# Batch 0 of a chunked attention kernel: dummy matmuls at TensorE's waits, memory values loaded by another queue, one pair of heads turned in another order

## The chip, the cores and the metric

The kernel runs on one core of a Trainium2 chip. The metric is the device time of one execution in microseconds, as the median over several executions. The core's engines run their own instruction streams and meet at semaphores: TensorE (PE in the profile, with its weight loads as PEld), VectorE (DVE), ScalarE (ACT), GpSimd (POOL) and SyncE (SP). POOL and SP issue the DMA transfers here, and sixteen DMA engines carry them.

## What is computed

Two stages follow each other. The first is attention in chunks of 32 queries for 4 batches and 8 heads of size 64, over 768 positions. Each chunk sees 8 memory rows, 16 positions to its left and 8 to its right. The second is a dense layer pair over all 3072 tokens with a sine activation between them.

```python
for c in range(24):                       # chunks of 32
    l, r = max(0, 32*c - 16), min(768, 32*c + 40)
    k_full = concat(mem_k, k[:, :, l:r]); v_full = concat(mem_v, v[:, :, l:r])
    a = softmax(q[:, :, 32*c:32*c+32] @ k_full.T / 8)
    out[:, :, 32*c:32*c+32] = a @ v_full
x = out as (3072, 512)                    # heads side by side
h = x @ w_in                              # 512 -> 2048
y = (h + sin(alpha * h)**2 / alpha) @ w_out   # 2048 -> 512
```

## The kernel before, in words

All instructions of an engine run in the order in which the program writes them; no scheduler moves them. The four batches go one after another, and the attention of a batch is woven with the second product of the batch before it (L517). Batch 0 has nothing to be woven with, so it has its own function, `attention_first`, and this is where the change lies.

Batch 0 works on pairs of heads, called pair 0 to 3 here (`hp` in the code). For each pair `turn_k` and `turn_q` put twelve TensorE transposes each (L234) into a PSUM bank. The keys are then copied to `kT` by ScalarE (L249, the middle) and VectorE (L242, the edges), the queries to `qT` by VectorE (L256). The eight memory keys of every head are turned once (L405), copied to `memkT` (L406) and spread over the windows of `kT` by `put_memk` (L200). `sc(hp)` makes the scores of a pair in two halves: in each, two matmuls write the mask (L328), eight add the products (L336), and ScalarE takes the exponential (L343). `pv` (L355) multiplies by the values in `vw`, VectorE normalizes (L361, L362), and `x` turns the result (L372), which ScalarE copies to `xT` (L375). `alphas` turns a small table (L601) and copies it (L602, L603). Then `ahead` begins the first dense product (L471).

`warm(n)` issues `n` matmuls of zeros, 128x512, into the bank that `single()` would hand out next (L323). PSUM has eight banks. At the start they are split by `plan`: ring `one` is bank 6 alone, ring `t` (the transposes) is banks 4, 5 and 7, ring `big` (scores) begins at banks 0 and 2. A ring with one bank hands out the same bank each time, so a `warm` waits until that bank has been read.

POOL issues nearly all loads, with conversion from fp32 to bf16, in this order: keys and queries of pairs 0 to 3, with the memory values of all four batches (`memv_st`, L564) between the queries of pair 2 and the keys of pair 3; then the edges of the value windows (L186, L187), the values of pairs 0 to 3 in two parts each (L180, L181), and `w_in` in five parts (L207), `w_out`, and batch 1's keys and queries. Completion semaphores go round in a ring of eight, so the n-th transfer that POOL issues waits for the landing of the one eight places ahead of it. SP issues the memory keys in fp32 (L552) and the alpha table (L553) at the start. Later, `send_memv(1)` has SP copy batch 1's memory values into its value windows by eight small transfers (L197), which wait for the landing of `memv_st`. `put_memv(0, ...)` does the same for batch 0 by one VectorE copy (L190).

Of the kernel before, what the change touches and what calls it, by code (L numbers as in the profile page):

```python
# [9 lines left out]
P = 128  # L10
# [4 lines left out]
F32 = mybir.dt.float32  # L15
# [27 lines left out]
def kernel(  # L43
# [12 lines left out]
    nc = tc.nc  # L56
    B, H, S, D = q.shape
# [15 lines left out]
    mlp = ctx.enter_context(tc.tile_pool(name="mlp", bufs=3))  # L73
# [7 lines left out]
    def plan(**sets):  # L81
        for kind, ring in sets.items():
            rings[kind] = list(ring)
# [14 lines left out]
    def single(kind="one"):  # L98
        return ps[:, take_bank(kind), :]

    def packed(bank, n, width):
        return bank.bitcast(BF)[:, 0:n * width].rearrange("p (n c) -> p n c", n=n)

    plan(one=(6,), big=(0, 2), t=(4, 5, 7))

    ident = consts.tile([P, P], BF, name="ident")
    biasm = consts.tile([P, 6], F32, name="biasm")
# [9 lines left out]
    memv_st = consts.tile([P, B, H, D], BF, name="memv_st")  # L117
# [54 lines left out]
    def load_v(b, parts=((0, H),)):  # L172
        vw = vws[b % 2][:].rearrange("p h j c -> p (h j) c")
        vf = v[b].rearrange("h (j t) d -> t (h j) d", t=QW)
        n = H * NJ
        if len(parts) > 1:
            load_v_edges(vw, vf, n)
        for h0, h1 in parts:
            c0, c1 = h0 * NJ, h1 * NJ
            nc.gpsimd.dma_start(vw[16:64, c0:c1, 0:D], vf[0:48, c0:c1])  # L180
            nc.gpsimd.dma_start(vw[72:120, c0:c1, 0:D], vf[48:96, c0:c1])  # L181
        if len(parts) == 1:
            load_v_edges(vw, vf, n)

    def load_v_edges(vw, vf, n):
        nc.gpsimd.dma_start(vw[0:16, 1:n, 0:D], vf[80:96, 0:n - 1])  # L186
        nc.gpsimd.dma_start(vw[120:128, 0:n - 1, 0:D], vf[0:8, 1:n])  # L187

    def put_memv(b, eng, h0, h1):
        eng.tensor_copy(  # L190
            vws[b % 2][64:72, h0:h1, :, 0:D],
            memv_st[64:72, b, h0:h1, :].unsqueeze(2).to_broadcast([NM, h1 - h0, NJ, D]),
        )
# [5 lines left out]
    def put_memk(b):  # L199
        nc.vector.tensor_copy(  # L200
            kTs[b % 2][:, :, 24:856].rearrange("p g (j c) -> p g j c", c=104)[:, :, :, 40:40 + NM],
            memkT[:, :, NM * b:NM * b + NM].unsqueeze(2).to_broadcast([P, HP, NJ, NM]),
        )
# [23 lines left out]
    def turn(src, hp, pr):  # L227
        t = packed(single("t"), 6, P)
        for r in range(6):
            if pr is not None:  # L230
                nc.tensor.transpose(t[:, r, :], pr[:, r].rearrange("p e d -> p (e d)"), ident[:])
            else:
                for e in range(2):
                    nc.tensor.transpose(  # L234
                        t[64 * e:64 * e + 64, r, :], src[:, 2 * hp + e, r, :], ident[:]
                    )
        return t

    def put_k_edges(b, hp, t):
        kT = kTs[b % 2]  # L240
        for t0, c0 in ((0, 16), (120, 800)):
            nc.vector.tensor_copy(  # L242
                kT[:, hp, c0:c0 + 48].rearrange("p (a r) -> p a r", r=6),
                t[:, :, t0:t0 + 8].rearrange("p r a -> p a r"),
            )

    def put_k(b, hp, t):
        kT = kTs[b % 2]
        nc.scalar.copy(  # L249
            kT[:, hp, 72:72 + 7 * 104].rearrange("p (s c) -> p s c", c=104)[:, :, 0:96]  # L250
            .rearrange("p s (a r) -> p s a r", r=6),
            t[:, :, 8:120].rearrange("p r (s a) -> p s a r", a=16),
        )

    def put_q(b, hp, t, scalar=False):
        (nc.scalar.copy if scalar else nc.vector.tensor_copy)(  # L256
            qTs[b % 2][:, hp, :].rearrange("p (a r) -> p a r", r=6),
            t.rearrange("p r a -> p a r"),
        )
# [60 lines left out]
    def warm(n):  # L320
        z = ps[:, rings["one"][0], :]
        for _ in range(n):
            nc.tensor.matmul(z, idle[:, 0:P], idle[:])  # L323

    def unit_scores(hp, half):
        sc = two()
        for e in range(2):
            nc.tensor.matmul(  # L328
                sc[:, e, 0:4 * QW].rearrange("p (j m c) -> p j m c", j=4, m=3), ident[:],
                biasb[:, half].unsqueeze(3).to_broadcast([P, 4, 3, 32]),  # L330
                start=True, stop=False,
            )
        for jj in range(4):
            j = 4 * half + jj
            for e in range(2):
                nc.tensor.matmul(  # L336
                    sc[:, e, QW * jj:QW * jj + QW],
                    kTs[0][64 * e:64 * e + 64, hp, 104 * j:104 * j + P],
                    qTs[0][64 * e:64 * e + 64, hp, QW * j:QW * j + QW],
                    start=False, stop=(jj == 3),  # L340
                )
        pt = pt_first[:, 2 * hp + half, :]
        nc.scalar.activation(  # L343
            pt[:, 0:H * QW].rearrange("p (e c) -> p e c", e=2), sc[:, :, 0:4 * QW],
            ACTF.Exp, scale=0.125,
        )
        return pt
# [21 lines left out]
    def unit_turn(xT, hp, half, x_blk):  # L369
        xtp = packed(single(), 4, QW)  # L370
        for jj in range(4):
            nc.tensor.transpose(  # L372
                xtp[:, jj, :], x_blk[:, jj].rearrange("p e d -> p (e d)"), ident[0:QW, 0:QW]
            )
        nc.scalar.copy(  # L375
            xT[:, hp, HALF * half:HALF * half + HALF].rearrange("p (j c) -> p j c", j=4), xtp
        )

    def attention_first(kq, alphas, ahead):
        xT = xp.tile([P, KT, S], BF, name="xT")  # L380
        pt, xb = {}, {}

        def turn_k(hp):
            t = turn(kq[0], hp, None)
            put_k(0, hp, t)
            put_k_edges(0, hp, t)

        def turn_q(hp):
            put_q(0, hp, turn(kq[1], hp, None))

        def sc(hp):
            for half in range(2):
                pt[hp, half] = unit_scores(hp, half)

        def pv(*u):
            xb[u] = unit_values(*u, pt[u])

        def x(*u):
            unit_turn(xT, *u, xb.pop(u))

        turn_k(0)
        turn_q(0)
        mt = packed(single(), HP, 32)
        for g in range(HP):
            nc.tensor.transpose(mt[:, g, :], memk_bf[0:32, 2 * g:2 * g + 2, :].rearrange("p e d -> p (e d)"), ident[0:32, 0:32])  # L405
        nc.vector.tensor_copy(memkT[:], mt)  # L406
        put_memk(0)
        warm(2)
        turn_k(1)
        sc(0)  # L410
        turn_q(1)
        alphas()
        warm(1)
        turn_k(2)
        sc(1)
        turn_q(2)
        put_memv(0, nc.vector, 0, H)
        turn_k(3)
        sc(2)
        turn_q(3)  # L420
        sc(3)
        nc.scalar.preload_act_table(ACTF.Sin)
        send_memv(1)
        plan(big=(4, 0, 2), one=(6, 7))
        units = [(hp, half) for hp in range(HP - 1) for half in range(2)]
        pv(0, 0)
        for n in range(1, len(units)):
            warm(1)
            pv(*units[n])
            warm(1)  # L430
            x(*units[n - 1])
        warm(1)
        pv(3, 0)
        x(2, 1)
        pv(3, 1)
        x(3, 0)
        ahead(0, 0, xT)
        ahead(1, 0, xT)
        x(3, 1)
        ahead(2, 0, xT)  # L440
        return xT
# [108 lines left out]
    alpha_rows = consts.tile([FT, P], F32, name="alpha_rows")  # L550
    for bb in range(B):
        nc.sync.dma_start(memk_f[NM * bb:NM * bb + NM], mem_k[bb].rearrange("h n d -> n h d"))  # L552
    nc.sync.dma_start(alpha_rows[:], moe_alpha.rearrange("(ft p) -> ft p", p=P))  # L553
    nc.vector.memset(idle[:], 0.0)
    warm(8)
    for vw in vws:
        nc.vector.memset(vw[0:32, 0, 0, 0:D], 0.0)  # L557
        nc.vector.memset(vw[96:128, H - 1, NJ - 1, 0:D], 0.0)
# [1 line left out]
    masks.make_identity(nc, ident[:])  # L560
    for hp in range(1, HP):
        load_qk(0, kq, 2 * hp, 2 * hp + 2)
        if hp == 2:
            nc.gpsimd.dma_start(memv_st[64:72].rearrange("n b h d -> n (b h) d"),  # L564
                                mem_v.rearrange("b h n d -> n (b h) d"))
    load_v(0, [(2 * hp, 2 * hp + 2) for hp in range(HP)])
    for kT in kTs:
        nc.vector.memset(kT[:, :, 0:16], 0.0)
        nc.vector.memset(kT[:, :, 848:856], 0.0)
# [17 lines left out]
    nc.vector.tensor_copy(biasb[:, 0, 0, 0:1], biasm[:, 3:4])  # L587
    nc.vector.tensor_copy(biasb[:, 1, 3, 2:3], biasm[:, 4:5])
    nc.vector.tensor_copy(memk_bf[:], memk_f[0:32])
    nc.vector.tensor_copy(ident_f[:], ident[0:FT, 0:FT])  # L590
    nc.vector.memset(pt_first[:, :, H * QW:H * QW + 32], 0.0)
    for pt in pts:
# [61 lines left out]
    for pc in range(2 * HP):  # L654
        hp = pc % HP
        if pc + 3 < 2 * HP:
            prs.append(pair_up(kq1[(pc + 3) // HP], (pc + 3) % HP))
        t = turn(None, hp, prs[pc])
# [74 lines left out]
```

## Time and profile before

| | us |
|---|---|
| median of 7 runs | 228.16 |
| lowest, highest | 227.99, 231.42 |
| the profiled execution, its time | 228.70 |
| its span, first to last instruction | 226.9 |
| TensorE busy in the span | 212.3 (94%) |
| start of batch 0's first transposes (L234) | 5.46 |
| start of its first scores (L328) | 9.34 |
| start of its first values (L355) | 20.93 |
| start of the first dense product (L471) | 28.19 |

Times inside the profile count from the first instruction. "Start" rows come from the timeline of TensorE's instructions. A row of the timeline gives the start, the length of the group, the engine, the line, what it writes and reads, how many instructions, and in brackets the idle time ahead of it with what ended it. A row of the table by windows gives, for a stretch of time, each engine's busy time with its number of instructions, then the mean clock that TensorE was granted (1.00 is full), the DMA share and the GB/s moved.

### The profile page before, as it was taken

Reading aid. Unit: us, or ns where it says so; the run is one execution under the profiler, and the core shown is the slowest. Engines: PE = TensorE matmul, PEld = TensorE weight load, DVE = VectorE, ACT = ScalarE, POOL = GpSimd, SP = SyncE. Lnnn points to the kernel's source line nnn. Section 1 sums busy time; section 2 is a strip of 40 time slices with the busy share of each in tenths; the row PEclk is TensorE's granted clock in tenths of the full one; section 3 lists DMA queues with packets and bytes.
Section 4 is the critical chain, followed back from the end, with each engine's and each line's share of the span. In section 5 each row is a group of like instructions: output and inputs, shape, how many; then the busy total and the mean of one; then the engine's idle time right before and its main releaser. Section 6 shows DMA issues by size and latency. Waiting matters only on the chain.

```text
span 226.9 us, 4419 instructions
## 1 busy us (share of the span) xinstructions
PE 212.3 (94%) x1703; PEld 115.2 (51%) x1703; DVE 135.2 (60%) x237; ACT 151.8 (67%) x222; POOL 84.4 (37%) x106
## 2 busy tenths in 40 slices
PE   6787899999998999999989999999999999999993
PEld 2354655554545656554555555554555555554441
DVE  5437938885615869996783577654853764762110
ACT  2367568894687749999865787798948678660011
POOL 8877926596989971168770000000000000000000
PEclk9799999999999999999999999999999999999999
DMA  5999999999999999999999954532330100102212
GB/s 81 149 140 127 198 207 209 204 199 121 69 184 150 155 132 120 161 123 171 162 174 104 83 105 93 103 108 92 71 111 0 49 20 26 46 16 82 92 46 92
DMA packets 94629, 25.96 MB, mean 114 GB/s; under 512 B 82688, under 2 KB 91536, under 8 KB 94608
## 3 DMA queue, kind: packets, MB, share of 16 engines
q0 software_dynamic: 71648, 14.82, 106.0%
q1 hardware_dynamic: 22960, 10.86, 22.9%
q8 instruction: 13, 0.21, 0.4%
q14 instruction: 8, 0.07, 0.2%
HBM read 29.67 MB, written 6.29 MB: 158 GB/s over the span
## 4 chain that ended last, share of the span: by engine, by line
PE 54%; DVE 8%; ACT 2%; issue 2%; DVEq 0%; ACTq 0%
PE ps L517 29%; PE ps L471 20%; DVE gT L501 3%; PE ps L270 2%; PE ps L296 2%; DVE u L498 2%; DVE x_blk L303 1%; ACT u L491 1%; PE ps L313 1%; ACT u L495 1%; DVE xT L316 1%; ACT o_sb L532 0%; DVE rinv L302 0%; DVE o_sb L530 0%; DVEq L501 0%
## 5 line engine op out<-in xcount | busy, mean ns | idle before, releaser
L517 PE MATMUL ps<-w_out_sb,gT 128*128 128x512 bf16 x384 | 99.2, 379 | 2.4 <-DVE o_sb L530 0.8
L471 PE MATMUL ps<-xT,w_in_sb 128*128 128x384 bf16 x512 | 90.0, 326 | 0.7 <-DVE gT L501 0.7
L501 DVE SCALAR_TENSOR_TENSOR gT<-u,inv_alpha,ps 128x768 bf16<-128x768 f32 x64 | 63.3, 1011 | 24.2 <-ACT u L495 20.1
L491 ACT ACTIVATE u<-ps,alpha_sb 128x768 f32<-128x768 f32 x64 | 57.0, 898 | 22.3 <-PE ps L471 21.2
L471 PEld LDWEIGHTS <-w_in_sb 128*128 128x128 bf16 x512 | 49.7, 98 | 37.5 <-issue 2.0
L517 PEld LDWEIGHTS <-gT 128*128 128x128 bf16 x384 | 34.3, 97 | 32.7 <-issue 2.7
L495 ACT ACTIVATE u<-u 128x768 f32<-128x768 f32 x40 | 33.7, 843 | 1.2
L283 ACT ACTIVATE pt<-ps,biasm 128x256 bf16<-128x256 f32 x72 | 28.7, 476 | 6.0 <-ACT pt L283 2.3
L530 DVE COPY o_sb<-ps 128x512 f32<-128x512 f32 x12 | 8.2, 687 | 24.5 <-PE ps L517 24.5
L532 ACT COPY o_sb<-ps 128x512 f32<-128x512 f32 x12 | 7.1, 588 | 22.2 <-PE ps L517 22.2
L498 DVE TENSOR_TENSOR u<-u 128x768 f32<-128x768 f32 x18 | 17.8, 988 | 6.0 <-ACT u L491 5.9
L303 DVE TENSOR_TENSOR x_blk<-ps,rinv 96x512 bf16<-96x512 f32 x24 | 16.5, 687 | 1.0 <-DVE rinv L302 0.2
L144 POOL DMA_DIRECT2D kst<-in_k_dram x16 | 11.7, 731 | 7.2 <-DMA vw<-in_v_dram 3.6
L139 POOL DMA_DIRECT2D kst<-in_k_dram x16 | 11.1, 693 | 7.8 <-DMA vw<-in_v_dram 6.2
L249 ACT COPY kT<-ps 128x672 bf16<-128x672 bf16 x8 | 5.8, 719 | 12.1 <-PE ps L234 8.6
L302 DVE RECIPROCAL rinv<-ps 96x8 f32<-96x8 f32 x24 | 4.9, 203 | 12.1 <-PE ps L296 6.2
L323 PE MATMUL ps<-idle 128*128 128x512 bf16 x22 | 8.7, 469 | 3.3 <-DVE vw L557 1.2
L498 POOL TENSOR_TENSOR u<-u 128x768 f32<-128x768 f32 x6 | 8.9, 1494 | 7.6 <-ACT u L491 7.6
L296 PEld LDWEIGHTS <-pt 128*128 128x128 bf16 x192 | 9.0, 98 | 4.8 <-issue 0.8
L152 POOL DMA_DIRECT2D qst<-in_q_dram x12 | 10.6, 898 | 1.4 <-DMA kst<-in_k_dram 1.2
L296 PE MATMUL ps<-vw,pt 128*128 128x65 bf16 x192 | 9.8, 193 | 0.0
L270 PEld LDWEIGHTS <-kT 64*128 64x128 bf16 x192 | 4.9, 94 | 7.6 <-issue 7.0
(76 smaller groups left out, 153.5 us busy)
## 6 DMA issues: line engine op xcount, KB each, us to landing
out_dram<-o_sb SPq DMA_DIRECT2D x24, 256.0 KB
vw<-in_v_dram POOLq DMA_DIRECT2D x6, 384.0 KB, 12.2
w_out_sb<-in_moe_w_out_dram POOLq DMA_DIRECT2D x2, 1024.0 KB, 17.7
w_in_sb<-in_moe_w_in_dram POOLq DMA_DIRECT2D x3, 512.0 KB, 9.6
qst<-in_q_dram POOLq DMA_DIRECT2D x12, 128.0 KB, 6.4
kst<-in_k_dram POOLq DMA_DIRECT2D x14, 64.0 KB, 5.3
kst<-in_k_dram POOLq DMA_DIRECT2D x14, 56.0 KB, 5.7
k_bf<-in_k_dram POOLq DMA_DIRECT2D x4, 192.0 KB, 5.5
```

Of the source, the lines that this page charges most:

```text
L139: nc.gpsimd.dma_start(kst[r0:64, j, :].rearrange("p (h d) -> p h d", d=D), k[b, :, lo + r0:lo + 64, :].rearrange("h p d -> p h d"),)
L144: nc.gpsimd.dma_start(kst[72:72 + n, j, :].rearrange("p (h d) -> p h d", d=D), k[b, :, QW * j + 48:QW * j + 48 + n, :].rearrange("h p d -> ...
L152: nc.gpsimd.dma_start(qst[:, t, :].rearrange("p (h d) -> p h d", d=D), q[b, :, P * t:P * t + P, :].rearrange("h p d -> p h d"),)
L283: nc.scalar.activation(pt[:, 0:H * QW].rearrange("p (g e c) -> p g e c", g=2, e=4)[:, :, :, 32 * m:32 * m + 32], sc[:, :, 0:4 * QW].rearra ...
L296: nc.tensor.matmul(otv[:, e, hp, :], pt[:, QW * i:QW * i + P], vws[b % 2][:, 2 * hp + e, j, 0:D + 1],)
L303: nc.vector.tensor_tensor(out=x_blk[:].rearrange("p g e d -> p e g d"), in0=otv[0:QW, :, :, 0:D], in1=rinv[:].unsqueeze(3).to_broadcast([Q ...
L471: nc.tensor.matmul(hT[:, hf, 0:HALF], w_in_sb[:, kt, P * ft:P * ft + P], xT[:, kt, HALF * hf:HALF * hf + HALF], start=(kt == 0), stop=(kt ...
L491: nc.scalar.activation(u[:], hT[:, :, 0:HALF], ACTF.Sin, scale=alpha_sb[:, ft:ft + 1])
L495: nc.scalar.activation(u[:], u[:], ACTF.Square)
L498: eng.tensor_tensor(out=u[:], in0=u[:], in1=u[:], op=ALU.mult)
L501: nc.vector.scalar_tensor_tensor(out=gT[:, ft, :].rearrange("p (e c) -> p e c", e=2), in0=u[:], scalar=inv_alpha[:, ft:ft + 1], in1=hT[:, ...
L517: nc.tensor.matmul(ps[:, bank, :], gT[:, ft, P * s:P * s + P], w_out_sb[:, ft, :], start=(ft == 0), stop=(ft == FT - 1),)
```

## The change

Four things change, all ahead of or in batch 0.

1. Ring `one` gets banks 6 and 7, and ring `t` keeps 4 and 5.
2. More `warm` calls: 11 at the start where there were 8; two after the first keys' transposes; three after `put_memk` where there were two; two ahead of the first scores; two after `alphas` where there was one; two after `turn_k(2)`; four after `turn_k(3)`; two ahead of the last scores.
3. SP loads the memory values of batch 0 as fp32 (`memv_f`, behind the memory keys and ahead of the alpha table), and VectorE converts them. POOL loads those of batches 1 to 3 behind the values. `put_memv(0)` stands behind `alphas` and no longer behind `turn_q(2)`.
4. The last pair's queries (`turn_q(3)`) are turned ahead of the scores of pair 2, and no longer behind them.

```diff
-    plan(one=(6,), big=(0, 2), t=(4, 5, 7))
+    plan(one=(6, 7), big=(0, 2), t=(4, 5))
...
         turn_k(0)
+        warm(2)
         turn_q(0)
         mt = packed(single(), HP, 32)
...
         put_memk(0)
+        warm(3)
+        turn_k(1)
         warm(2)
-        turn_k(1)
         sc(0)
         turn_q(1)
         alphas()
-        warm(1)
+        put_memv(0, nc.vector, 0, H)
+        warm(2)
         turn_k(2)
+        warm(2)
         sc(1)
         turn_q(2)
-        put_memv(0, nc.vector, 0, H)
         turn_k(3)
+        warm(4)
+        turn_q(3)
         sc(2)
-        turn_q(3)
+        warm(2)
         sc(3)
...
         nc.sync.dma_start(memk_f[NM * bb:NM * bb + NM], mem_k[bb].rearrange("h n d -> n h d"))
+    memv_f = mlp.tile([P, H, D], F32, name="memv_f", tag="o_sb", bufs=2)
+    nc.sync.dma_start(memv_f[64:72], mem_v[0].rearrange("h n d -> n h d"))
     nc.sync.dma_start(alpha_rows[:], moe_alpha.rearrange("(ft p) -> ft p", p=P))
     nc.vector.memset(idle[:], 0.0)
-    warm(8)
+    warm(11)
...
     for hp in range(1, HP):
         load_qk(0, kq, 2 * hp, 2 * hp + 2)
-        if hp == 2:
-            nc.gpsimd.dma_start(memv_st[64:72].rearrange("n b h d -> n (b h) d"),
-                                mem_v.rearrange("b h n d -> n (b h) d"))
     load_v(0, [(2 * hp, 2 * hp + 2) for hp in range(HP)])
+    nc.gpsimd.dma_start(memv_st[64:72, 1:B].rearrange("n b h d -> n (b h) d"),
+                        mem_v[1:B].rearrange("b h n d -> n (b h) d"))
...
     nc.vector.tensor_copy(memk_bf[:], memk_f[0:32])
+    nc.vector.tensor_copy(memv_st[64:72, 0], memv_f[64:72])
     nc.vector.tensor_copy(ident_f[:], ident[0:FT, 0:FT])
```

## The prediction, as it was put on record

> **What bounds the kernel now.** I read the page first, for TensorE's share and its clock; then TensorE's timeline up to the first dense product; then the table by windows over that stretch; then the issues of each transfer, one by one, with their time to landing. The page says that TensorE is 94% busy over the span and that the only slices below full clock are at its head:
>
> ```profile
> PE   6787899999998999999989999999999999999993
> PEclk9799999999999999999999999999999999999999
> ```
>
> So after batch 0 the kernel is a chain of dense matmuls, and a change in batch 0 is worth what it moves the start of that chain (28.19 us). In the table by windows, cut where the clock changes, the reader is to see one stretch of 3.41 us at half clock, behind a stretch of equal length in which TensorE was busy for only 1.95 us:
>
> ```profile
> core 0: us, PE busy (x) PEld busy (x) DVE busy (x) ACT busy (x) POOL busy (x), PEclk, DMA share, GB/s
> 0.00:5.45 5.45, 3.59 (x8) 1.01 (x8) 3.08 (x24) 1.28 (x1) 4.32 (x11) 1.00 0.55 79
> 5.45:8.86 3.41, 1.95 (x36) 1.27 (x38) 2.52 (x14) 0.72 (x1) 3.41 (x6) 1.00 1.14 156
> 8.86:12.27 3.41, 3.41 (x44) 1.71 (x40) 0.32 (x2) 1.98 (x3) 2.52 (x4) 0.50 1.23 148
> 12.27:15.68 3.41, 2.43 (x40) 1.23 (x36) 1.61 (x5) 1.55 (x3) 2.84 (x5) 1.00 2.63 144
> ```
>
> TensorE's own timeline shows the idle places, with what ended each:
>
> ```profile
> 8.15 0.59 PE L323 MATMUL ps<-idle 128*128 128x512 bf16 x2 [1.00 <-DVE memkT L406]
> 8.68 0.73 PE L234 MATMUL ps<-ident,k_bf 128*64 128x128 bf16 x12
> 13.62 0.38 PE L323 MATMUL ps<-idle 128*128 128x512 bf16 x1 [0.98 <-DVE alpha_sb L602]
> 13.92 0.53 PE L234 MATMUL ps<-ident,k_bf 128*64 128x128 bf16 x12
> 17.38 0.35 PE L336 MATMUL ps<-qT,kT 64*128 64x96 bf16 x8 [0.29 <-DVE qT L256]
> 19.94 0.35 PE L336 MATMUL ps<-qT,kT 64*128 64x96 bf16 x8 [0.62 <-DVE qT L256]
> 20.93 0.42 PE L355 MATMUL ps<-vw,pt_first 128*128 128x65 bf16 x8
> ```
>
> The two waits of about 1.0 us are zero matmuls that wait for their single bank to be read (memkT, alpha_sb), and everything is queued behind them. Landings, as issue plus time to landing, in us: keys of pair 1 3.40+4.6 = 8.0, queries of pair 1 4.12+6.1 = 10.2, keys 2 4.83+6.5 = 11.3, queries 2 5.54+7.1 = 12.6, keys 3 6.93+6.4 = 13.3, queries 3 7.64+7.2 = 14.8; second parts of the values: pair 0 11.66+7.1 = 18.8, pair 1 13.63+8.4 = 22.0, pair 2 15.10+8.4 = 23.5, pair 3 17.71+6.8 = 24.5; first part of w_in 18.91+6.6 = 25.5, second 19.66+7.1 = 26.8.
>
> **The change part by part.** Unit prices from the timeline, start to start at full clock: twelve transposes 0.46 (13.92 to 14.38), followed directly by others 0.37 to 0.43; a pair's scores 1.41 (14.38 to 15.79); a zero matmul 0.21 (21.18 to 21.39 between values). At half clock the scores took 2.37 (9.34 to 11.71).
>
> *Start.* The first eight zero matmuls are 0.427 apart (weight loads at 2.02, 2.45, 2.88, 3.30, 3.73). Eleven put the last at 1.19 + 10 x 0.427 = 5.46, just when the first keys land; they then start at about 5.7 instead of 5.46 (0.4 late if the last three run slow). Keys 0 5.7, two zero matmuls 6.1, queries 0 6.55 (landed at 6.34), memory keys 7.0, three zero matmuls 7.2: these no longer wait for memkT, because ring `one` has a second bank. They end at 7.85, and keys 1 start at their landing, 8.0 against 8.68.
>
> *VectorE beside it.* It gets one cast more, of 8 partitions x 512; its nearest row is the memk_bf cast of the same length, 0.53. At 5.8 it pushes the key edges from 6.78 to 7.3, the query copy (0.95) to 7.5, memkT to 8.4 and put_memk to 8.6, done at 8.95. Scores 0 need that at 9.33 (below), and keys 1, which now share a bank with keys 0, need the edges done by 8.0: covered by 0.4. The cast waits for SP's transfer. SP's queue shows memory keys and alpha moved by 5.5 (the last three packets of its queue lie in 5.0 to 5.5); the new transfer takes alpha's place, so I take no wait; the far bound is the 6.6 us that POOL's memory values took to land, 2.2+6.6 = 8.8.
>
> *Middle.* Keys 1 8.0, zeros 8.45, scores 0 8.9 to 10.3, queries 1 (landed 10.2) 10.3, alpha 10.75, zeros 10.95, keys 2 (landed 11.3) 11.36 against 13.92. Of these 2.56 us, 0.7 come from the memkT wait, about 1.2 from the clock (0.96 on scores 0, 0.24 on queries 1), and 1.0 from the alpha wait, less the zeros put in. Zeros 11.8, scores 1 12.25 to 13.65, queries 2 13.65, keys 3 14.1, four zeros 14.5, queries 3 15.36, scores 2 15.8 to 17.2, zeros, scores 3 17.65 to 19.06. From keys 2 on the stretch grows from 7.0 to 7.7: eight zeros cost 1.7, and the waits of 0.29 and 0.62 with their restarts go. No step waits: put_memv (1.22) now runs on VectorE at about 12.1 to 13.35, ahead of the key edges of pair 2 (to 13.6), which keys 3 need at 14.1 for the bank; the query copies end at 11.8, 15.1 and 16.8, needed at 12.7, 15.8 and 18.1; ScalarE's exponentials (0.76 each) keep pace. put_memv may hold up POOL's descriptor work for half a microsecond, as it did before (the issue beside it took 1.20, the others 0.73); POOL then waits for landings anyway.
>
> *Clock: a rule weighed.* The windows show the half clock behind a stretch with no idle gap above 1.00 us and 57% busy, and full clock kept behind 2.43 of 3.41 (71%). The Trainium skill, "TensorE: Matmul & The Clock Gate", section "Why this matters for your kernels", asks only that no idle gap be over about 3 us. By that rule the clock would not have fallen here at all, so zeros would buy no clock; the trace contradicts it, and I go with the trace. The same page's Part 4 says that transposes do not count as busy in the same way. That speaks against the change: counted so, the stretch before the fall had the 0.59 of zeros, and the one that kept the clock 2.43 less 0.9 of transposes, 1.5. The changed stretch has 0.2+0.43+0.64+0.4 = 1.7 without transposes, and over 3.2 with them: above both kept values. If the clock falls for one stretch all the same, scores 0 and queries 1 cost 1.2 more and the gain at the values is 0.6.
>
> *Loads and values.* POOL's order loses the 0.73 us issue of memory values ahead of keys 3, and each later transfer waits for the one eight ahead in the new count, so the first value parts go out some 1.4 earlier. But DMA has been full since 4 us (share above 1), so landings follow traffic. Ahead of pair 1's values go away 256 rows of memory values and SP's eight small copies (8 x 64 rows, issued 12.88 to 18.85, now behind the later load); 64 rows come in. Six value parts of 768 rows landed between 18.8 and 24.5: 1.24 ns a row, so 704 rows are 0.87 us. Pair 1's values then land at 21.1, within bounds of 20.9 and 22.0. Values 0 start at 19.06 (landed by 18.8), and pair 1's follow 1.84 later as before: 20.9 wanted, 21.1 had. So late next is a landing, by 0.2, and the gain at 22.76 is 1.65 (0.75 if no traffic is saved). The values of pairs 2 and 3 have 1.3 and 2.1 us before, and follow.
>
> *Behind it.* VectorE's pace of 0.85 to 1.07 a unit is unchanged, so the dense product starts near 26.6. w_in part 1 lands at 25.5 plus up to 0.6 for the copies now beside it (26.1); part 2 at 27.4, wanted at about 28.4. Batch 1's keys land at 48.4, wanted on POOL at 50.93, then 49.3; its queries at 52.6, wanted at 56.26; its values at 62.8 at the latest, wanted at 67.94. None is late by an advance of 1.6.
>
> Sum: 1.65 less a little lost in the chain, 1.5 us. The profiled execution took 228.70 with a span of 226.9; it would be 227.2. Its time is 0.54 above the median of the seven, so the median goes from 228.16 to 226.7.
>
> **The rivals.**
> *The landings bind.* If SP's copies and memory values took no DMA time from the values, pair 1 lands at 22.0 and the gain is 0.75: 227.4. For it: share well above 1 at 13 to 22 us, with many transfers under way; against: GB/s fall to about 80 to 120 while the copies are issued.
> *The clock falls still, or falls at another place.* Its stretches need not lie at the same places in other executions. Gain 0.6: 227.5. Two such stretches: none, 228.7.
> *Slower: VectorE's queue stops at the new cast.* If memv_f lands late, the key edges, the query copy, memkT and put_memk wait, with them keys 1 and scores 0. From 6.2 on it eats the slack, at 7.8 the gain is gone, and at the 8.8 of the far bound scores 0 start 2.2 to 2.5 late with TensorE idle and the clock at half behind it (1.2): about 230.3. Against: the packets of SP's queue.
> *More than the sum.* The chain of values gains from the early activation-table load, and landings leave no wait: 2.3 or more, below 225.9.
> *That it does not act* is excluded by the order: the two waits are gone from the instructions.
>
> **How the numbers follow.** Sum 0.55, landings 0.15, clock 0.12, slower 0.07, more 0.11. What a measurement here tells from no change is about 1%, 2.28 us: faster means below 225.9, slower above 230.4. The sum and the first two rivals lie within it. So faster 0.11, same 0.83, slower 0.06. The range leaves out half of the faster case and the slower one: 225.9 to 228.2.
>
> **What would show it.** Right: granted clock 1.00 from 5.5 on; zeros directly behind the memory keys; keys 2 near 11.4; first values near 19.1; the dense product near 26.6. Wrong: an idle place on VectorE ahead of the new cast; a window at 0.50; values of pair 1 waiting for a DMA by more than 0.5; L471 waiting for w_in.

## The result and the profile after

| | before | changed |
|---|---|---|
| median of the comparison, us | 229.07 (61 runs) | 227.40 (24 runs) |
| lowest to highest | 227.98 to 231.69 | 226.78 to 228.44 |
| the profiled execution | 228.70 | 228.50 |

The ratio of changed to before is 0.9921, with a 95% interval of 0.9900 to 0.9943: 1.8 us less on 229. A second comparison gave medians of 228.70 and 227.21 and a ratio of 0.9955 (0.9938 to 0.9972). There, the ratio leaves out those runs of the kernel before that lie more than 1.5% above its fastest (226.56), so it is nearer to 1 than the medians are; both are given below.

The two profiles differ by only 0.2 us, since the changed kernel's is of an execution longer than all 24 of the comparison. Its profile still shows what the change did. First the table by windows of the changed kernel, cut where it was cut before:

```profile
core 0: us, PE busy (x) PEld busy (x) DVE busy (x) ACT busy (x) POOL busy (x), PEclk, DMA share, GB/s
0.00:5.45 5.45, 4.26 (x11) 1.49 (x11) 3.09 (x24) 1.28 (x1) 4.33 (x11) 1.00 0.53 78
5.45:8.86 3.41, 3.41 (x41) 1.60 (x41) 2.93 (x14) 0.72 (x1) 3.41 (x6) 1.00 1.17 166
8.86:12.27 3.41, 3.41 (x53) 1.75 (x51) 1.49 (x5) 2.24 (x3) 2.66 (x4) 1.00 1.18 157
12.27:15.68 3.41, 3.41 (x60) 2.03 (x61) 3.00 (x7) 2.51 (x4) 2.22 (x3) 1.00 3.07 129
```

TensorE is busy throughout, and no window is recorded at half clock. Then lines of TensorE's timeline, for the places that were idle before and for what is idle now:

```profile
6.00 0.85 PE L234 MATMUL ps<-ident,k_bf 128*64 128x128 bf16 x12
...
7.77 0.26 PE L406 MATMUL ps<-ident,memk_bf 32*128 32x32 bf16 x4
7.97 0.82 PE L323 MATMUL ps<-idle 128*128 128x512 bf16 x3
8.72 0.53 PE L234 MATMUL ps<-ident,k_bf 128*64 128x128 bf16 x12
...
12.18 0.53 PE L234 MATMUL ps<-ident,k_bf 128*64 128x128 bf16 x12
...
20.64 0.40 PE L355 MATMUL ps<-vw,pt_first 128*128 128x65 bf16 x8 [0.59 <-DMA vw<-in_v_dram]
...
27.79 1.70 PE L476 MATMUL ps<-xT,w_in_sb 128*128 128x384 bf16 x8
```

The zeros follow the memory keys without a wait (7.97), the second wait is gone too, and keys 2 start at 12.18 where they started at 13.92. But the first keys start at 6.00 and take 0.85 where they took 0.53, which is the duration at half clock (the last section shows how the record can miss it), and the first values wait 0.59 us for a landing. Of the 1.74 us that keys 2 had gained, 0.4 are left at the dense product (27.79 against 28.19).

### The profile page after: what moved, and what is told of

It reads as the page before. It is cut to its first block, busy times and chain, and to the rows that moved or that the text cites. A ratio compares the mean times of both kernels' runs of the same rounds, so it can differ in the third digit from the quotient of the medians.

```text
span 226.7 us, 4455 instructions
## 1 busy us (share of the span) xinstructions
PE 215.5 (95%) x1720; PEld 116.2 (51%) x1720; DVE 135.6 (60%) x238; ACT 151.7 (67%) x222; POOL 84.2 (37%) x106
## 4 chain that ended last, share of the span: by engine, by line
PE 40%; DMA 26%; POOL 13%; SPq 8%; issue 5%; DVE 4%; ACT 2%; POOLq 1%; DVEq 0%; ACTq 0%
PE ps L522 21%; DMA vw<-in_v_dram 17%; PE ps L476 14%; DMA kst<-in_k_dram 8%; SPq L159 4%; POOL qst L152 4%; SPq L162 4%; POOL kst L144 2%; DVE gT L506 2%; POOL kst L139 2%; POOL q_bf L167 1%; ACT u L496 1%; POOL k_bf L167 1%; DMA out_dram<-o_sb 1%; POOL vw L180 1%
## 5 line engine op out<-in xcount | busy, mean ns | idle before, releaser
L503 DVE TENSOR_TENSOR u<-u 128x768 f32<-128x768 f32 x18 | 17.2, 954 | 6.0 <-ACT u L496 5.9
L323 PE MATMUL ps<-idle 128*128 128x512 bf16 x39 | 13.9, 452 | 1.2 <-DVE vw L564 1.2
L152 POOL DMA_DIRECT2D qst<-in_q_dram x12 | 10.5, 902 | 0.8 <-DMA kst<-in_k_dram 0.8
## 6 DMA issues: line engine op xcount, KB each, us to landing
w_out_sb<-in_moe_w_out_dram POOLq DMA_DIRECT2D x2, 1024.0 KB, 18.6
```

The lines of the kernel that those rows point to most:

```text
L152: nc.gpsimd.dma_start(qst[:, t, :].rearrange("p (h d) -> p h d", d=D), q[b, :, P * t:P * t + P, :].rearrange("h p d -> p h d"),)
L503: eng.tensor_tensor(out=u[:], in0=u[:], in1=u[:], op=ALU.mult)
```

## The experiments

Each kernel ran beside the kernel before on one chip. "Mean clock" is the granted clock averaged over an execution; one stretch of 3.4 us at half clock makes it 0.992, since 1.7 of 227 us are lost. It does not count a head at half clock that lies ahead of the first recorded change (last section).

### Each part alone or left out

**The memory values alone** (part 3 of the change, nothing else).

```diff
+    nc.sync.dma_start(memv_f[64:72], mem_v[0].rearrange("h n d -> n h d"))
...
-        put_memv(0, nc.vector, 0, H)      # behind turn_q(2)
+        put_memv(0, nc.vector, 0, H)      # behind alphas()
```

> The kernel before with the memory-value edits alone (part 3 of the change). Theory A (the gain comes from TensorE's filled waits and its clock; the loads' new order gives nothing by itself): the half-clock stretch behind the first transposes stays, first values start at about 20.9 as before, pair 0's values land near 20.5 because more transfers share the DMA engines; time within 0.3 us of the kernel before, ratio 0.998 to 1.002. Theory B (the freed DMA traffic brings the values and through them the time): first values earlier by 0.5 or more and the time 0.9 us shorter, ratio 0.996.

Measured: median 229.73 against 228.99, ratio 1.005 (1.0018 to 1.0082). Both theories fall: it costs. Eight of its runs have a mean clock of 0.991 to 0.993, and the shortest of them (228.95) is longer than the longest of the twenty such runs of the kernel before (228.81). VectorE's timeline of this kernel:

```profile
5.26 0.53 DVE L590 CAST memk_bf<-memk_f 32x512 bf16<-32x512 f32 x1
5.82 0.69 DVE L591 CAST memv_st<-memv_f 8x512 bf16<-8x512 f32 x1
6.52 0.45 DVE L592 CAST ident_f<-ident 16x16 f32<-16x16 bf16 x1
...
8.43 0.20 DVE L406 COPY memkT<-ps 128x128 bf16<-128x128 bf16 x1
```

The new cast does not wait for its data, but it took 0.69 us where I had taken 0.53, and the small copy behind it 0.45 where it had taken 0.15. memkT is copied at 8.43 and not at 7.88, and the zeros, and keys 1 behind them, still wait for it. This looks like the cause, but the profile does not show it. In this execution the first queries are turned at half clock (0.85 for twelve transposes, 0.51 more up to the memory keys), so that their copy, which stands ahead of memkT's, could hardly have begun earlier. The kernel with the second bank alone (below) has no such cast, was profiled with the same half clock, and copies memkT later still:

```profile
8.51 0.21 DVE L406 COPY memkT<-ps 128x128 bf16<-128x128 bf16 x1
```

Keys 2 start at 14.89 here and at 13.92 in the kernel before, and nearly all of that is the half clock: 0.51 up to the memory keys, 0.53 on the zeros and keys 1. From keys 2 to the first values both take 7.0. Where the head runs at full clock, as in the profile of the kernel without the last six zeros (below), the cast does delay that copy: it starts 0.48 behind its transposes, against 0.06 in the kernel before. So about 0.4 us is an estimate of what the cast can cost while keys 1 wait for memkT; that it makes up the 0.5% is likely and not shown. The values do come earlier (pair 1's second part was issued at 12.54 and took 7.4 us: 19.9 against 22.0 before), but TensorE was not waiting for them.

**Everything but the memory values** (parts 1, 2 and 4).

```diff
-    nc.sync.dma_start(memv_f[64:72], mem_v[0].rearrange("h n d -> n h d"))
-    nc.vector.tensor_copy(memv_st[64:72, 0], memv_f[64:72])
...
+        if hp == 2:
+            nc.gpsimd.dma_start(memv_st[64:72].rearrange("n b h d -> n (b h) d"),
+                                mem_v.rearrange("b h n d -> n (b h) d"))
```

> The changed kernel without the memory-value edits: zeros, second bank and the order of the last queries alone. Theory A: clock at 1.00 throughout, put_memv now late on VectorE and in front of the last query copy (scores 3 about 0.5 later), pair 0's values land near 19 as before the change, pair 1's at 22.0; the gain over the kernel before is 0.75 to 1.8 us, ratio 0.992 to 0.997. Theory B (the memory-value edits carry the gain): ratio 0.998 to 1.000.

Measured: 227.12 (six runs, 226.67 to 227.38), ratio 0.9920 (0.9890 to 0.9949). All of the gain is there without part 3. Mean clock 0.997 or more in all six. In its profile pair 0's values landed at 20.0 and the first values wait 0.57 us for them, so this wait does not come from part 3 alone.

**The second bank alone** (part 1).

```diff
-    plan(one=(6,), big=(0, 2), t=(4, 5, 7))
+    plan(one=(6, 7), big=(0, 2), t=(4, 5))
```

> The kernel before with the second bank for the ring of single banks alone (the two waits of 1 us on the copies go, no zeros are added). Theory clock (what counts is that TensorE is kept busy so that its clock is not halved): the stretch of half clock of about 3.4 us is still there, scores 0 still take 2.4, and the gain is under 0.8 us, ratio 0.9965 or more. Theory waits (what counts are the waits of 1.0 and 0.98 themselves): keys 2 start 1.0 to 1.7 us earlier than 13.92 and the gain is 1.5 us or more, ratio 0.9935 or less.

Measured: 227.39 (226.12 to 229.47), ratio 0.9923 (0.9897 to 0.9949). One line brings as much at the median as the whole change, although the mean clock is 0.992 or lower in 15 of its 22 runs. From its timeline of TensorE:

```profile
7.52 0.28 PE L405 MATMUL ps<-ident,memk_bf 32*128 32x32 bf16 x4
7.74 1.03 PE L323 MATMUL ps<-idle 128*128 128x512 bf16 x2
8.70 0.85 PE L234 MATMUL ps<-ident,k_bf 128*64 128x128 bf16 x12
...
12.10 0.53 PE L234 MATMUL ps<-ident,k_bf 128*64 128x128 bf16 x12
...
19.83 0.40 PE L355 MATMUL ps<-vw,pt_first 128*128 128x65 bf16 x8 [0.67 <-DMA vw<-in_v_dram]
```

In this execution the keys of pair 1 still run at half clock (0.85), yet keys 2 start at 12.10, 1.82 us earlier than before and no later than in the changed kernel. The waits account for it: from the memory keys to the zeros behind them it is 0.22 where it was 1.26, and from alpha to keys 2 0.48 where it was 1.51, together 2.07 less. The half clock lies elsewhere in the two executions, earlier in this one, and takes back 0.25: 1.18 more up to scores 0, 0.93 less on scores 0 and queries 1. The reader should also see the last line: here too the first values wait for a landing, though this kernel's loads are those of the kernel before.

**The zeros alone** (part 2 with the single bank and the old order).

```diff
-    warm(8)
+    warm(11)
...
+        warm(2)                 # behind turn_k(0)
...
-        warm(2)
+        warm(3)                 # behind put_memk(0)
         turn_k(1)
+        warm(2)
...
-        warm(1)
+        warm(2)                 # behind alphas()
         turn_k(2)
+        warm(2)
...
+        warm(4)                 # behind turn_k(3)
...
+        warm(2)                 # ahead of sc(3)
```

> The kernel before with all the new zero matmuls, but with its single bank for them and its old order, so that the two waits of 1 us on the copies stay. Theory clock (the zeros' worth is a clock that does not fall): the mean granted clock of nearly every run is 0.995 or more where the kernel before has 0.992 or 0.978 in 32 of 43 runs, and the ratio is 0.992 to 0.997. Theory waits (the worth lies in the bank that takes the two waits away, the zeros are load on TensorE's path): ratio 0.998 or more, the zeros behind the last keys and ahead of the last scores showing as about 1 us more between keys 2 and the first values.

Measured: 229.37 against 228.70, ratio 1.0044 (1.0026 to 1.0061). The mean clock was 0.995 or more in 22 of 22 runs, as the clock theory said, and the time got longer, as the other said. Over all runs the means are 229.27 and 229.05: the zeros narrow the spread (228.33 to 229.93, against 226.56 to 231.56) and do not lower the middle. TensorE's timeline has both old waits in it, and zeros that come on top:

```profile
8.38 0.81 PE L323 MATMUL ps<-idle 128*128 128x512 bf16 x3 [0.99 <-DVE memkT L407]
...
13.08 0.59 PE L323 MATMUL ps<-idle 128*128 128x512 bf16 x2 [0.97 <-DVE alpha_sb L607]
13.61 0.53 PE L234 MATMUL ps<-ident,k_bf 128*64 128x128 bf16 x12
...
16.70 1.04 PE L323 MATMUL ps<-idle 128*128 128x512 bf16 x4
```

Keys 2 start at 13.61, only 0.3 earlier than before, with the clock whole; then the zeros behind keys 3 take 0.9 (16.70 to 17.58).

**Everything but the new zeros** (parts 1, 3 and 4, with the old 8, 2 and 1).

> The changed kernel with only the zeros that the kernel before has (8, 2 and 1). Theory clock: the clock falls in part of the runs (means of 0.992 or less in a third or more of them), the spread between lowest and highest is 2.5 us or more as with the ring alone (226.1 to 229.5), and the median is 227.2 to 228. Theory waits: no loss against the changed kernel, median 226.0 to 226.9, since its path is shorter by the zeros.

Measured: 226.99 (226.40 to 229.20, 16 runs); the changed kernel beside it 227.21. Ratio 0.9960 (0.9934 to 0.9986), median against median 226.99/228.70 = 0.9925. The mean clock fell to 0.988 to 0.992 in 5 of 16 runs, and the spread is 2.8 us. So the zeros do keep the clock whole and the runs together, but they do not shorten the median. In the execution profiled the first values wait 1.28 us for pair 0's landing, so there a shorter path of TensorE could not show.

### Fewer zeros, and the changed kernel again

**Without the last six** (four behind keys 3, two ahead of scores 3).

```diff
-        warm(4)
         turn_q(3)
         sc(2)
-        warm(2)
         sc(3)
```

> The changed kernel without the four zero matmuls behind the last keys and the two ahead of the last scores. Theory landing (in the changed kernel the first values wait for pair 0's landing at about 20.5, 0.6 us of wait in the profile): scores 3 end about 1 us earlier, the wait grows by as much, time same as the changed kernel within 0.3 us, ratio to before 0.991 to 0.9935. Theory TensorE (its own queue of work ends last): the first values come 0.9 to 1.3 earlier, ratio to before 0.987 or less.

Measured: 226.74 (226.59 to 227.37, six runs), ratio 0.9909 (0.9880 to 0.9939). In its profile the first values start at 19.02 with no wait, and pair 0's values had landed at 18.6. Neither theory holds as stated: the time is 0.7 below the changed kernel's 227.40, or 0.3 by the two ratios to the kernel before, and not 1.2, and the landing was not late in this execution. Leaving out six zeros, about 1.3 us of work, shortened the stretch from keys 2 to the first values by only 0.4 (11.60 to 19.02 here, 12.11 to 19.90 in the second profile of the changed kernel), since other waits take their place, the longest ahead of queries 3:

```profile
15.48 0.53 PE L234 MATMUL ps<-ident,q_bf 128*64 128x128 bf16 x12 [0.72 <-DVE qT L256]
```

**Zeros only where TensorE waits anyway.**

```diff
-    warm(11)
+    warm(10)
...
         turn_k(1)
-        warm(2)
         sc(0)
...
         turn_k(2)
-        warm(2)
         sc(1)
...
-        warm(4)
         turn_q(3)
         sc(2)
-        warm(2)
```

> The changed kernel with zeros only where TensorE has to wait for a landing or a copy anyway: ten at the start (the last then ends as the first keys land), two behind the first keys, three behind the memory keys, two behind alpha, none ahead of scores 0, 1, 3 and none behind the last keys. If the zeros that fill no wait are pure load: 226.1 to 226.6, ratio 0.987 to 0.990, clock 0.995 or more in all runs. If they are needed for the clock: means of 0.992 in part of the runs and a median of 226.9 or more.

Measured: 226.87 (226.16 to 228.36), ratio 0.9906 (0.9880 to 0.9932), median against median 0.9920; the changed kernel beside it 227.21. The two ratios, 0.9906 and 0.9955, are further apart than these medians, which are 0.34 us apart. 21 of 22 runs have a mean clock of 0.995 or more, so those few zeros hold the clock. The median is above my 226.1 to 226.6. The execution profiled is one of the longest (228.19) and shows two waits, 1.06 us ahead of the first values for pair 0's landing and 1.05 at 153.12 (see "Behind it" below); how much of them is in the median is not shown.

**The changed kernel once more.**

> The changed kernel as it is, beside the others on one chip, with a second profile. Its first profile was one of its slowest executions: first keys still at half clock, pair 0's values landed at 20.5 and TensorE waited 0.59 us for them. If these two are what makes its runs differ, a profile at about 227.2 shows first keys at full clock, keys 2 near 11.6 and pair 0's values landing by 19.5 with first values at 19.2 to 19.8; if landing is always late, the wait of about 0.6 is there again with first values at 20 or later.

Measured: 227.21 (226.71 to 227.72, 22 runs). In this profile pair 0's second part went out at 10.46 and took 9.0 us: landed at 19.46, first values at 19.90 without a wait, dense product at 27.16. The first keys are at 6.00 again. So the late start is the same in both profiles and the late landing is not. The late start is not fixed either: with the same eleven zeros, the profiles of the zeros alone and of the kernel without the last six have the first keys at 5.57 and 5.58, at full clock (0.53).

### The landing

In both profiles of the changed kernel pair 0's values are issued earlier than before and land later. These are the DMA issues of the kernel before and then of the changed kernel, each for a stretch in which only this transfer is issued; the last figure is the time to landing:

```profile
vw<-in_v_dram POOLq DMA_DIRECT2D x1, 96.0 KB, 7.1
```

```profile
vw<-in_v_dram POOLq DMA_DIRECT2D x1, 96.0 KB, 10.5
```

Issued at 11.66 it landed at 18.8; issued at 10.01 it landed at 20.5. An early issue alone does not do it: with the memory values alone this part was issued at 10.52 and landed at 18.6. Nor does it take the new loads: with the second bank alone, 11.24 and 19.7. If rows that lie ahead of it in the queue delay it, then taking some away should help. The edges of the value windows are 1512 rows for all pairs, of which pair 0 needs a quarter.

```diff
         if len(parts) > 1:
-            load_v_edges(vw, vf, n)
+            load_v_edges(vw, vf, n, 0, n // 2)
         for h0, h1 in parts:
+            if 2 * h0 == H:
+                load_v_edges(vw, vf, n, n // 2, n)
```

> The kernel with zeros only at the waits, and with the edges of the value windows loaded in two halves: those of pairs 0 and 1 ahead of pair 0's values, those of pairs 2 and 3 behind pair 1's. It takes 756 of 1512 edge rows out of the traffic ahead of pair 0's values and adds two issues on the load queue. Theory landing (the first values of the changed kernel wait for pair 0's landing at 19.5 to 20.5, and rows ahead of it are what delays it): pair 0 lands at 18.5 to 19.0, the wait of 1.06 us ahead of the first values is under 0.4, median 225.9 to 226.4 against 226.87. Theory sharing (transfers under way at the same time share the DMA engines, so that an earlier place in the queue brings nothing): landing and wait as before, median 226.7 to 227.1.

Measured: 226.18 (225.84 to 226.75, six runs) against 229.11, ratio 0.9893 (0.9856 to 0.9929). Pair 0 landed at 18.05 (issued 9.75, 8.3 to landing). Where the kernel with the same zeros but whole edges has the first line, this one has the second:

```profile
19.62 0.40 PE L355 MATMUL ps<-vw,pt_first 128*128 128x65 bf16 x8 [1.06 <-DMA vw<-in_v_dram]
```

```profile
18.52 0.42 PE L359 MATMUL ps<-vw,pt_first 128*128 128x65 bf16 x8
```

The wait of 1.06 us is gone, and the median is 0.7 lower, though measured on another chip; the intervals of the two ratios overlap (0.9893 here, 0.9906 there), so the gain in time is not shown.

**The same with the old memory values.**

> The same with the memory values loaded and copied as in the kernel before, so without the new cast on VectorE and with SP's small copies again beside the values. If the memory-value edits bring the values earlier: pair 0's values land 0.5 to 1 us later than with them and the median is 0.4 to 0.8 us above the one with them. If they bring nothing: the same within 0.3 us.

Measured: 225.85 (225.21 to 226.41, six runs), ratio 0.9882 (0.9847 to 0.9917), the shortest of all here. Without part 3 the time is, if anything, shorter. Pair 0 landed at 18.5 (issued 11.11, 7.4 to landing). The two landings with split edges lie below all ten profiles with whole edges, 18.6 to 20.5. In its profile the next wait is the one that the prediction had looked for and not found in the changed kernel, the first part of w_in:

```profile
26.78 1.47 PE L476 MATMUL ps<-xT,w_in_sb 128*128 128x384 bf16 x8 [0.77 <-DMA w_in_sb<-in_moe_w_in_dram]
```

| kernel | median | before, same runs | ratio (95%) |
|---|---|---|---|
| second bank alone | 227.39 | 228.99 | 0.9923 (0.9897 to 0.9949) |
| zeros alone | 229.37 | 228.70 | 1.0044 (1.0026 to 1.0061) |
| memory values alone | 229.73 | 228.99 | 1.0050 (1.0018 to 1.0082) |
| whole change, second comparison | 227.21 | 228.70 | 0.9955 (0.9938 to 0.9972) |
| bank, order, few zeros, split edges | 225.85 | 229.11 | 0.9882 (0.9847 to 0.9917) |

## Why the prediction was right, and where its reasons were not

**The total.** 1.5 us less was forecast; the medians of the two comparisons differ by 1.67 and 1.49. 226.7 against 227.40 is mostly the kernel before, whose median was 229.07 over 61 runs and not 228.16 as over seven. That the sum came out is in part luck: the lead was to be 2.56 at keys 2 and 1.6 at the dense product, and the two profiles had 1.74 and 1.81, then 0.40 and 1.03. What the parts below lost came back in places that the prediction had not named, and in runs of the kernel before that were longer than the one it was read from.

**The waits on one bank: right.** Both are gone, and the second bank alone carries the gain (0.9923). I had booked 0.7 and 1.0 for them; the bank alone took 2.07 from them, 1.82 at keys 2.

**The clock: the mechanism right, its worth wrong.** The term "about 1.2 from the clock" was read from one execution as if every one had that half-clock stretch and lost that much by it. The zeros do keep the recorded clock (0.996 or more in all 47 executions of the changed kernel), but added alone they made the kernel 0.4% slower. The runs of the kernel before with just one such stretch are, by their median, its shortest (below). The limit between 57% and 71% busy was read from one execution, and no run here tests it. And the filler has its price, though less than "eight zeros cost 1.7" suggests: leaving out six brought 0.4 on TensorE's path, since VectorE's copies then set the pace.

**The start: mis-sized.** I had the first keys at 5.7. Eleven zeros that are all at half clock (0.427 each) end at 5.9, and the keys behind them can be at half clock as well: 6.00 in both profiles, with 0.85 and 0.79 for twelve transposes. This is most of the 0.8 by which keys 2 (12.18) missed the forecast 11.36.

**The new cast: the price was low, the cover held.** It took 0.69 and not 0.53. Part 3 alone costs 0.5%, and whether through the cast is not shown; in the changed kernel nothing on TensorE waits for it, since keys 1 no longer stand behind memkT. The rival in which VectorE stops for a late transfer did not occur: there is no idle time ahead of the cast.

**The landings: a step that failed.** "Values 0 start at 19.06 (landed by 18.8)" took an earlier issue and less traffic to mean a landing no later than before. It was 20.5 and 19.5 in the two profiles, with time to landing up from 7.1 to 10.5 and 9.0. What came late was pair 0; I had expected it of pair 1. That rows ahead of it are part of the cause fits the two profiles with split edges, which land below all others; with so few, and times that overlap, it is not settled. Why the same transfers land a microsecond apart in two executions of one kernel stays open. So does the worth of the 0.87 us of freed traffic: leaving part 3 out made no difference that these runs can tell (227.12 against 227.40 and 227.21).

**Behind it: right for the loads it named, incomplete for the rest.** w_in was in time, but the lead at the dense product is not what arrives at the end. In the second profile it is 1.03 at 27.16, 1.64 at 118, and 1.2 at the end, 0.4 of it going behind the last copy. The gain on the way is a wait of the kernel before that shrinks from 0.78 to 0.15:

```profile
51.32 4.48 PE L517 MATMUL ps<-w_out_sb,gT 128*128 128x512 bf16 x20 [0.78 <-DVE gT L501]
```

In the first profile it is 0.40, then 1.01 at 119, then 0.60 at 167 (and 0.2 at the end), since a new wait appears (a row of VectorE's timeline and one of TensorE's):

```profile
151.77 0.69 DVE L535 COPY o_sb<-ps 128x512 f32<-128x512 f32 x1 [2.90 <-DMA out_dram<-o_sb]
153.44 0.35 PE L270 MATMUL ps<-qT,kT 64*128 64x96 bf16 x8 [0.34 <-DVE gT L506]
```

VectorE waits for a buffer that an output transfer has yet to empty. SP issued that transfer at 149.44, behind its transposes for batch 3; in the second profile it did so at 145.43, and TensorE has no wait there. The same wait is 1.05 with zeros only at the waits and 0.60 with the edges split. From the first dense product to the end, the twelve profiles take 197.8 to 199.6 us, a range as large as the whole gain. Why SP is late in some executions stays open.

## What to carry to other kernels

Before filling a wait with dummy work, ask what the dummy work itself waits for: a ring with one bank made the filler wait for a copy, and a second bank was worth more than all the filler. Filler that stands where nothing waits is load on the path, and only an experiment with each part alone tells the two apart. When an engine stops waiting, look at what comes next as well: here the landing of the first values (18.6 to 20.5 in ten profiles with whole edges), then the first part of w_in, then an output transfer far behind. A lead at one place is worth what is left of it at the end.

## What the runs showed of the hardware

**One kernel, three clock histories.** In one comparison of 43 runs the kernel before had a mean clock of 0.991 or 0.992 in 20 runs (median 228.30), 0.978 or lower in 12 (230.63), and 0.995 or more in 11 (229.41). The clock is granted and taken back at moments that differ between executions, and the times, which spread over 3.5 us in all, fall into groups with it. The mean clock does not order them, though: in the comparison of 69 runs, those at 0.997 to 0.999 are either the shortest (seven, 226.56 to 227.44) or the longest (nine, 231.18 to 231.56), and the shortest are as short as the changed kernel's (226.71 to 227.72). So what the change takes away is above all the long runs. Its own mean clock was 0.996 or more throughout, and its 24 runs lie within 1.7 us. A mean just below 1 need be no loss: in its first profile (0.997) the recorded fall lies behind 224 us, after the last matmul.

**A granted clock of 1.00 is not proof of full clock at the head.** The page of the kernel with the memory values alone shows full clock in every slice, while its first transposes took what half clock takes:

```profile
PEclk9999999999999999999999999999999999999999
```

```profile
5.46 0.85 PE L234 MATMUL ps<-ident,k_bf 128*64 128x128 bf16 x12 [0.68 <-DMA k_bf<-in_k_dram]
...
9.62 0.85 PE L234 MATMUL ps<-ident,k_bf 128*64 128x128 bf16 x12
...
14.89 0.53 PE L234 MATMUL ps<-ident,k_bf 128*64 128x128 bf16 x12
```

Twelve transposes take 0.85 us until about 13 us and 0.53 from then on, with no change in the row of the clock. That 0.85 is half clock can be worked out from the kernel before, where the stretch at half clock is recorded: keys 1 start 0.18 us ahead of it and take 0.66 from start to start, which fits 0.46 at full clock and 0.78, as here (9.62 to 10.40), at half. Its first eight zeros, too, stand 0.427 apart under a clock given as 1.00, and later ones take 0.21. That may also be why a mean of 1.00 need not be a short run: the record seems to begin with the first change, and a head at half clock ahead of it is not counted. The durations of one kind of instruction are the safer reading.
